# Scores of the last eight attention units: two insertions of 32-row matmuls become one of 64-row matmuls, with halves of q and k moved between row groups by ScalarE copies

## The chip, the cores and the metric

The kernel runs on one core of a Trainium2 chip. The metric is device time in microseconds (us): the median of the executions of one program. A profiled execution gives a trace of each engine: TensorE (PE for matmuls, PEld for the loads of their stationary operand), VectorE (DVE), ScalarE (ACT), GpSimd (POOL), and SyncE (SP), which issues most of the loads. ScalarE issues DMAs too (ACTq).

## The reference

Three layers in a row, all in float32: attention within chunks of 64 positions, an RMS norm with a gated MLP (512 to 1536 to 512), and a second MLP (512 to 2048 to 512). There are 8 x 576 = 4608 tokens of 8 heads x 64.

```python
def _attn_ref(q, k, v):                       # (8, 8, 576, 64) each
    scores = scale * np.matmul(q_c, k_c.transpose(0, 1, 2, 4, 3))
    scores = scores - np.max(scores, axis=-1, keepdims=True)
    attn = np.exp(scores)
    attn = attn / (np.sum(attn, axis=-1, keepdims=True) + 1e-09)
    out = np.matmul(attn, v_c)
...
def _moe_ref(x, w_gate, w_val, w_out, rms_g):
    xn = x / np.sqrt(np.mean(x * x, axis=-1, keepdims=True) + 1e-06) * rms_g
    g = xn @ w_gate
    silu = g * (1.0 / (1.0 + np.exp(-g)))
    return silu * (xn @ w_val) @ w_out
...
def _moe2_ref(x, w_in, w_out):
    h = x @ w_in
    return (h * np.clip(h + 3.0, 0.0, 6.0) / 6.0) @ w_out
```

## The kernel before

**Stages.** The 4608 tokens are nine blocks of 512. The first stage computes the first MLP for blocks 0 to 2; the second (it begins at 379 us) does it for blocks 3 to 8, two blocks at a time; the third is the second MLP. Every large matmul is made of three matmuls on a high and a low part of the operands: the high part is a ScalarE cast (a "cast" below), the low part a VectorE or GpSimd subtraction of it from the original.

**A pair of blocks in the second stage.** A pair first goes through the *product part*. Its gate and value matrices are multiplied by a scheme of seven products of sums and differences of blocks in place of eight. The products of one group of hidden columns are written as slots (pr, m): product pr from 1 to 7 and half m, 0 or 1. A slot is six matmuls of `product` (line 1034 in the trace). The order of slots in a group is (1,0), (1,1), then (4,·) and (3,·) of the group before, (5,·) and (6,·), and at the end (2,0), (7,0), (2,1), (7,1). The first group has no (4,·) and (3,·). The accumulation banks of a group are read ("evacuated") behind certain slots:
- (6,0) and (6,1): ScalarE copies, lines 1433 and 1436. These are the two evacuations that the prediction speaks of ahead of the activation.
- (2,0): ScalarE's Silu activation, line 1353. Slot (1,0) of the next group overwrites the bank that it reads.
- (7,0): a ScalarE copy (1444), a VectorE addition, and a Silu after the next slot. (7,1): a ScalarE copy (1449) and a VectorE addition.
- (2,1): a VectorE multiply on the bank (line 1362 as all of these additions and multiplies): the "late multiply". Slot (1,1) of the next group overwrites that bank.

After six groups the *second part* of the pair follows: 24 items of 12 matmuls each by w_out (`mm_down_a`), whose operands are split by a ScalarE cast and a GpSimd subtraction (lines 1357 and 1358) two items ahead.

**Attention in between.** While one pair is computed, the attention of the following blocks is put in between. A unit of attention is 256 tokens of all heads. The second stage has eight (`Wide`, indices 10 to 17), four under each of the first two pairs. Unit n of a pair begins at 0, 14, 28 or 42 ticks after the pair's start; a pair has 66 ticks. A *tick* is two slots (12 matmuls, 2.74 us at the spacing of the trace) or one item. At each tick the kernel's own agenda (`at`, `tick`) runs the steps that are due then, so each engine's order of instructions is the order in which the program's lines run. The steps and their ticks are in the table `STEPS_P` (line 43). Units 1 and 5 begin in their pair's first group: `turn_q` is run behind slot (1,1), `turn_k` behind (5,1), and steps of ticks 2 and 3 behind (6,1) and (2,1) (this group ends with (2,0), (2,1), (7,0), (7,1)). Units 2, 3, 6 and 7 begin in a later group: `turn_q` behind (3,1), `turn_k` behind (6,0), and steps of ticks 2 and 3 behind (6,1) and (7,0). What is due at tick 5 lies behind the first slots of the group that follows.

**The steps of a unit.** `turn_q` and `turn_k` are one VectorE transpose of 32 x 32 blocks each (`turned`, line 908; 128 rows x 1024 elements). Of a head's 64 features, the transposed tile holds features 0 to 31 of a head (g = 0) in one half of its columns and 32 to 63 (g = 1) in the other half, on the same 32 rows. So a score, a sum over 64 features, is two accumulating matmuls on 32 rows (`start=g == 0`, `stop=g == 1`). `scores0` and `scores1` insert 32 such calls each between product matmuls; in the trace a call counts as two records, line 928. `top0` and `top1` take the maxima (VectorE, line 939), then come `less`, `expo`, `total`, `share`, a transpose of the result, `values`, and the squares for the norm.

The units of the first stage (`Pair`, the base class) have q and k loaded in another layout and make their scores in one insertion of 32 calls on 64 rows (line 799).

**Beside the units** the same queues hold: the sums and differences of the block operands (VectorE, lines 1252 and 1248, and ScalarE casts 1245, "xt" and "xu"); a preparation of weights for the third stage (`Raw`: loads "sraw" issued on ScalarE's queue, line 248; an activation, VectorE bit operations 256, 257, 262, 265; the cast of line 277 to "shi" or "sc"; the subtraction 278 on GpSimd; and stores to a stash, lines 296 and 300, on ScalarE's queue); and the RMS norm of a finished block (lines 957 to 984), which falls into units 3 and 7.

**Temporaries.** xt, sc, shi, slo and s3 share one pool, `tmp_p`, of four buffers of 128 x 512, taken in turn. A tile that takes a buffer waits until everything that uses the buffer's tile before is done.

## Time and profile before

| What | Value |
|---|---|
| Median of three runs | 1682.11 us (1678.25, 1682.11, 1682.73) |
| Profiled execution | 1679.51 us |
| Its span in the trace | 1677.7 us |
| TensorE matmuls | 1649.2 us, 98% of the span, 9920 records |
| VectorE | 1086.8 us, 65% |
| ScalarE | 845.2 us, 50% |
| GpSimd | 459.5 us, 27% |
| Mean granted TensorE clock | 0.995 of full speed |

The span is the time from the first to the last instruction in the trace; the execution's own time is 1.8 us longer. A timeline row gives a start, a duration, the engine and the program's line; in brackets stands how long the engine had stood idle before it, and which instruction released it. Rows of the same kind that follow each other are joined, and "x" counts them. Matmuls overlap, so the spacing of starts tells what one of them costs TensorE, not its duration.

### The profile page before, as it was taken

Reading aid. Unit: us, or ns where it says so; the run is one execution under the profiler, and the core shown is the slowest. Engines: PE = TensorE matmul, PEld = TensorE weight load, DVE = VectorE, ACT = ScalarE, POOL = GpSimd, SP = SyncE. Lnnn points to the kernel's source line nnn. Section 1 sums busy time; section 2 is a strip of 40 time slices with the busy share of each in tenths; the row PEclk is TensorE's granted clock in tenths of the full one; section 3 lists DMA queues with packets and bytes.
Section 4 is the critical chain, followed back from the end, with each engine's and each line's share of the span. In section 5 each row is a group of like instructions: output and inputs, shape, how many; then the busy total and the mean of one; then the engine's idle time right before and its main releaser. Section 6 shows DMA issues by size and latency. Waiting matters only on the chain.

```text
span 1677.7 us, 26541 instructions
## 1 busy us (share of the span) xinstructions
PE 1649.2 (98%) x9920; PEld 1350.7 (81%) x9920; DVE 1086.8 (65%) x1600; ACT 845.2 (50%) x1409; POOL 459.5 (27%) x336
## 2 busy tenths in 40 slices
PE   8999999999999999999999999999999999999998
PEld 7777888878878888788887888888788878887886
DVE  6998566656575775758436378448746764874475
ACT  6786344455454454645434344455445544654552
POOL 1001434321326522364226622131023003301310
PEclk8999999999999999999999999999999999999999
DMA  9913777747876488855979766667767786777665
GB/s 301 271 37 71 207 208 222 205 152 251 292 262 224 168 297 286 290 176 185 361 238 316 293 239 226 213 190 250 219 209 224 209 243 191 223 218 235 189 200 150
DMA packets 336096, 375.07 MB, mean 224 GB/s; under 512 B 184288, under 2 KB 260064, under 8 KB 335840
## 3 DMA queue, kind: packets, MB, share of 16 engines
q1 hardware_dynamic: 273984, 302.84, 58.4%
q10 hardware_dynamic: 61984, 70.53, 12.2%
q8 instruction: 79, 1.29, 0.3%
q14 instruction: 49, 0.40, 0.1%
HBM read 292.55 MB, written 80.74 MB: 223 GB/s over the span
## 4 chain that ended last, share of the span: by engine, by line
PE 45%; DVE 5%; DMA 1%; ACT 1%; issue 1%; SPq 1%; DVEq 0%; POOL 0%; ACTq 0%; POOLq 0%
PE PS L1034 24%; PE PS L1584 13%; PE PS L1023 2%; DVE gs L1578 1%; PE PS L1051 1%; PE PS L1048 1%; PE PS L1049 1%; DVE gt L1720 1%; PE PS L1056 1%; PE PS L1057 1%; PE PS L1060 1%; SPq L1603 1%; DMA stash_in<-sc 1%; PE PS L1784 1%; DVE oq L1598 0%
## 5 line engine op out<-in xcount | busy, mean ns | idle before, releaser
L1034 PE MATMUL PS<-xu,wo 128*128 128x512 f32 x1512 | 353.1, 392 | 3.4 <-DVE gu L1362 2.3
L1034 PEld LDWEIGHTS PS<-xu,wo 128*128 128x128 f32 x1512 | 282.3, 188 | 65.0 <-DVE gu L1362 3.1
L1034 PE MATMUL PS<-xo,wq 128*128 128x512 f32 x1344 | 305.3, 389 | 0.0
L1584 PE MATMUL PS<-gs,wq 128*128 128x512 f32 x1296 | 296.2, 390 | 2.4 <-DVE gs L1578 2.0
L1034 PEld LDWEIGHTS PS<-xo,wq 128*128 128x128 f32 x1344 | 252.3, 188 | 52.4
L1584 PEld LDWEIGHTS PS<-gs,wq 128*128 128x128 f32 x1296 | 242.7, 188 | 55.3 <-DVE gs L1578 5.0
L1023 PE MATMUL PS<-XH,w 128*128 128x512 f32 x576 | 148.9, 401 | 5.1 <-ACT sg L1331 3.1
L1023 PEld LDWEIGHTS PS<-XH,w 128*128 128x128 f32 x576 | 108.0, 191 | 29.2 <-ACT sg L1331 3.8
L1048 PE MATMUL PS<-gs,wd 128*128 128x512 f32 x288 | 113.4, 394 | 1.6 <-DVE gu L1362 1.6
L1049 PE MATMUL PS<-gs,wd 128*128 128x512 f32 x288 | 112.2, 390 | 0.0
L1079 POOL TENSOR_TENSOR al<-sg,ah 128x512 fp32r<-128x512 f32 x40 | 56.2, 1404 | 156.2 <-ACT ah L1077 151.9
L1358 POOL TENSOR_TENSOR gs<-gu,gs 128x512 fp32r<-128x512 f32 x60 | 86.6, 1461 | 42.7 <-ACT gs L1357 33.9
L1651 POOL TENSOR_TENSOR gt<-gx 128x512 f32<-128x512 f32 x8 | 10.3, 1289 | 299.8 <-DVE gx L1648 299.8
L1362 DVE TENSOR_TENSOR gu<-gu,PS 128x512 f32<-128x512 f32 x60 | 41.0, 685 | 77.4 <-ACT gu L1444 42.0
L1578 DVE TENSOR_TENSOR gs<-gu,gs 128x512 fp32r<-128x512 f32 x88 | 67.9, 792 | 31.4 <-ACT gs L1577 31.1
L1577 ACT CAST gs<-gt 128x512 fp32r<-128x512 f32 x96 | 58.3, 623 | 49.6 <-DVE gt L1720 44.3
L1515 DVE SCALAR_TENSOR_TENSOR gu<-gu,PS 128x512 f32<-128x512 f32 x48 | 32.8, 684 | 72.6 <-ACT gu L1512 72.6
L1023 PE MATMUL PS<-XL,w 128*128 128x512 f32 x288 | 78.9, 396 | 0.0
L1077 ACT CAST ah<-sg 128x512 fp32r<-128x512 f32 x52 | 32.3, 621 | 88.9 <-DVE sg L1335 63.2
L1051 PE MATMUL PS<-gs,wd 128*128 128x512 f32 x288 | 77.0, 389 | 0.0
L1577 ACT CAST gs<-gu 128x512 fp32r<-128x512 f32 x96 | 57.2, 621 | 22.8 <-DVE gs L1578 15.6
L1651 POOL TENSOR_TENSOR gt<-gu 128x512 f32<-128x512 f32 x24 | 32.5, 1355 | 129.0 <-DVE gu L1648 124.9
(251 smaller groups left out, 2887.6 us busy)
## 6 DMA issues: line engine op xcount, KB each, us to landing
wq<-stash_in SPq DMA_DIRECT2D x128, 512.0 KB
wo<-ops SPq DMA_DIRECT2D x126, 512.0 KB
wq<-sums_out SPq DMA_DIRECT2D x64, 512.0 KB
wq<-stash_out SPq DMA_DIRECT2D x48, 512.0 KB
wd<-keep_out SPq DMA_DIRECT2D x36, 512.0 KB
yd<-yst SPq DMA_DIRECT2D x18, 512.0 KB
ops<-w ACTq DMA_DIRECT2D x36, 256.0 KB
v<-in_v_dram SPq DMA_DIRECT2D x32, 256.0 KB
```

The lines of the kernel that those rows point to most:

```text
L1023: nc.tensor.matmul(ps, w(wi, c), xs[c][xi], start=(i == 0), stop=(i == n - 1))
L1034: nc.tensor.matmul(PS[:, bank, :], op[:, wi, c * 128:(c + 1) * 128], x[xi][:, c, :], start=first and i == 0, stop=last and i == 5, skip_gr ...
L1048: nc.tensor.matmul(ps, wm[0], a[0], start=first, stop=False)
L1049: nc.tensor.matmul(ps, wm[1], a[0], start=False, stop=False)
L1051: nc.tensor.matmul(PS[:, banks[m], :], w[:, 0, m * 128:(m + 1) * 128], a[1], start=False, stop=last)
L1079: nc.gpsimd.tensor_tensor(lo, t, hi.bitcast(F32), op=ALU.subtract)
L1358: nc.gpsimd.tensor_tensor(w[:, 1, :], t, w[:, 0, :].bitcast(F32), op=ALU.subtract)
L1362: nc.vector.tensor_tensor(o, x, y, op=op)
L1577: nc.scalar.copy(w[:, 0, :], x)
L1578: e.tensor_tensor(w[:, 1, :], x, w[:, 0, :].bitcast(F32), op=ALU.subtract)
L1584: nc.tensor.matmul(PS[:, banks[m], :], op[:, wi, m * 128:(m + 1) * 128], x[xi], start=first and (wi, xi) == (0, 0), stop=False, skip_group ...
L1651: nc.gpsimd.tensor_tensor(slot(i, "t"), slot(i, "12"), slot(i, "11"), op=ALU.subtract)
```

## The change

In the eight units a head's halves g = 0 and g = 1 are put on 64 neighbouring rows, so that a score is one matmul on 64 rows.

- `turned` makes three transposes of 128 x 512 in place of one of 128 x 1024: g = 1 into the second half of the target's columns, g = 0 into the first half, and g = 0 again into a new tile `half` from the pool `tmp_p`.
- `move_q` and `move_k` (new steps, ticks 2 and 3 of a unit) then make four ScalarE copies of 32 rows x 512 each: for each 64-row group, the lower rows' g = 1 goes to the upper rows' first half of columns, and the upper rows' g = 0 (from `half`, since that place in the target has just been overwritten) goes to the lower rows' second half.
- `scores` is one step at tick 5 (before, two steps at ticks 3 and 5): 32 calls on 64 rows. `top` is one maximum over all heads (that of the class `Pair`, line 809), in place of two over half of them.

The diff:

```diff
@@ -43,8 +43,9 @@
 STEPS_P = (
     (0, ("turn_q",)),
     (1, ("turn_k",)),
-    (3, ("scores0", "top0")),
-    (5, ("scores1", "top1")),
+    (2, ("move_q",)),
+    (3, ("move_k",)),
+    (5, ("scores", "top")),
     (6, ("less",)),
     (7, ("expo",)),
     (9, ("total", "share")),
@@ -905,43 +906,46 @@
                         yield
 
         def turned(self, to, x):
-            nc.vector.transpose(
-                out=to.rearrange("p (h g t u) -> p h u g t", h=2, g=2, u=8),
-                in_=x.rearrange("p (h u g f) -> p h u g f", h=2, u=8, g=2),
-            )
-
-        def scores(self, e):
+            self.moved = tmp_p.tile([128, 512], F32, tag="tmp", name="half")
+            for o, g in ((to[:, 512:1024], 1), (to[:, 0:512], 0), (self.moved, 0)):
+                nc.vector.transpose(
+                    out=o.rearrange("p (h t u) -> p h u t", h=2, u=8),
+                    in_=x.rearrange("p (h u g f) -> p h u g f", h=2, u=8, g=2)[:, :, :, g],
+                )
+
+        def move(self, to, moved):
+            for j in range(2):
+                lo, hi = slice(j * 64, j * 64 + 32), slice(j * 64 + 32, (j + 1) * 64)
+                nc.scalar.copy(to[hi, 0:512], to[lo, 512:1024])
+                nc.scalar.copy(to[lo, 512:1024], moved[hi, :])
+
+        def turn_q(self):
+            super().turn_q()
+            self.moved_q = self.moved
+
+        def move_q(self):
+            self.move(self.qT, self.moved_q)
+
+        def move_k(self):
+            self.move(self.kT, self.moved)
+
+        def scores(self):
             ps = PS[:, ATT:ATT + 2, :].rearrange("p z (t e c k) -> p z t e c k", t=2, e=2, c=2)
             self.s = PS[:, ATT:ATT + 2, :].rearrange("p z (x k) -> p z x k", k=CH)
             qT, kT = (
-                x.rearrange("p (h g n) -> p g h n", h=2, g=2) for x in (self.qT, self.kT)
+                x.rearrange("p (e h t c n) -> p h e t c n", e=2, h=2, t=2, c=2) for x in (self.qT, self.kT)
             )
             for t in range(2):
-                for y in range(2):
-                    for g in range(2):
-                        for h in range(2):
-                            for j in range(2):
-                                c = h ^ y
-                                f = slice((2 * j + e) * 32, (2 * j + e + 1) * 32)
-                                n = slice((2 * t + c) * 64, (2 * t + c + 1) * 64)
-                                x = side(2 * h + e, j)
-                                nc.tensor.matmul(
-                                    ps[x * 64:(x + 1) * 64, h, t, e, c, :],
-                                    qT[f, g, h, n],
-                                    kT[f, g, h, n],
-                                    start=g == 0,
-                                    stop=g == 1,
-                                )
-
-        def top(self, e):
-            if e == 0:
-                self.mx = sm_p.tile([128, 2, 2 * NP], F32, tag="mx", name="mx")
-            nc.vector.tensor_reduce(
-                out=self.mx.rearrange("p z (t e c) -> p z t e c", t=2, e=2)[:, :, :, e],
-                in_=self.s.rearrange("p z (t e c) k -> p z t e c k", t=2, e=2)[:, :, :, e],
-                axis=AX.X,
-                op=ALU.max,
-            )
+                for a, c, j in FOURS:
+                    f = slice(j * 64, (j + 1) * 64)
+                    x = side(a, j)
+                    nc.tensor.matmul(
+                        ps[x * 64:(x + 1) * 64, a // 2, t, a % 2, c, :],
+                        qT[f, a // 2, a % 2, t, c, :],
+                        kT[f, a // 2, a % 2, t, c, :],
+                        start=True,
+                        stop=True,
+                    )
 
     XN = {}
 
```

In what follows, the lines of the changed kernel stand 1 to 4 further down than those of before.

VectorE, the first ticks of unit 5, before (1252 and 1248 make operands, 908 is the turn, 1362 the late multiply, 939 the maximum):

```order
L1252 TENSOR_TENSOR xt<-xf 128x512
L908 STREAM_TRANSPOSE qT<-q 128x2x8x64
L1248 TENSOR_TENSOR xu<-xt,xu 128x512
L1252 TENSOR_TENSOR xt<-xf 128x512
L908 STREAM_TRANSPOSE kT<-k 128x2x8x64
L1248 TENSOR_TENSOR xu<-xt,xu 128x512 x2
L256 TENSOR_SCALAR sc<-sc 128x512
L257 TENSOR_SCALAR sc<-sc 128x512
L1362 TENSOR_TENSOR ge<-ge,PS 128x512
L939 TENSOR_REDUCE mx<-PS 128x4x2
```

VectorE, the same place, after:

```order
L1256 TENSOR_TENSOR xt<-xf 128x512
L911 STREAM_TRANSPOSE qT<-q 128x2x8x32 x2
L911 STREAM_TRANSPOSE half<-q 128x2x8x32
L1252 TENSOR_TENSOR xu<-xt,xu 128x512
L1256 TENSOR_TENSOR xt<-xf 128x512
L911 STREAM_TRANSPOSE kT<-k 128x2x8x32 x2
L911 STREAM_TRANSPOSE half<-k 128x2x8x32
L1252 TENSOR_TENSOR xu<-xt,xu 128x512 x2
L257 TENSOR_SCALAR sc<-sc 128x512
L258 TENSOR_SCALAR sc<-sc 128x512
L1366 TENSOR_TENSOR ge<-ge,PS 128x512
```

Each turn has become three transposes in a row, and the maximum (939) behind the multiply is gone from here.

ScalarE at unit 5, before, with what each row waits for by semaphore (1433 and 1436 are the evacuations of (6,0) and (6,1), 1353 the activation of (2,0), 255 an activation of the weights' preparation):

```order
L1245 CAST xu<-xt 128x512 [waits DVE_49] x2
L277 CAST shi<-sraw 128x512 [waits DMAHW6_49,DMAHW5_49]
L248 DMA sraw<-in_moe_w_out_dram 128x1024 [waits DMAHW1_49]
L1433 COPY gu<-PS 128x512 [waits PE_49]
L1436 COPY s_6104<-PS 128x512 [waits PE_49]
L1245 CAST xu<-xf 128x512
L255 ACTIVATE sc<-sraw 128x512 [waits DMAHW7_49,DMAHW2_49,DVE_49]
L1353 ACT_TABLE_LOAD
L1353 ACTIVATE ge<-PS 128x512 [waits PE_49]
```

ScalarE, the same place, after:

```order
L1249 CAST xu<-xt 128x512 [waits DVE_49] x2
L278 CAST shi<-sraw 128x512 [waits DMAHW7_49,DVE_49]
L249 DMA sraw<-in_moe_w_out_dram 128x1024 [waits DMAHW2_49]
L1437 COPY gu<-PS 128x512 [waits PE_49]
L1440 COPY s_6034<-PS 128x512 [waits PE_49]
L919 COPY qT<-qT 32x512
L920 COPY qT<-half 32x512 [waits Activation_49]
L919 COPY qT<-qT 32x512
L920 COPY qT<-half 32x512 [waits Activation_49]
L1249 CAST xu<-xf 128x512
L256 ACTIVATE sc<-sraw 128x512 [waits DMAHW3_49,Activation_49]
L1357 ACT_TABLE_LOAD
```

The four copies of `move_q` stand between the evacuation 1440 and the cast of an operand, ahead of the activation of (2,0), whose table load is the last row here. The cast `shi` now waits for a semaphore of VectorE.

ScalarE at unit 7, before (965 is the norm's square root, 300 the stores to the stash, 1444 the copy of (7,0)):

```order
L965 ACT_TABLE_LOAD
L965 ACTIVATE rt<-PS,eps 128x512 [waits PE_49]
L300 DMA stash_out<-sc 128x2x256 [waits DMAHW7_49,Activation_49]
L300 DMA stash_out<-slo 128x2x256 [waits DMAHW0_49,Pool_49]
L1353 ACT_TABLE_LOAD [waits DMAHW2_49]
L1353 ACTIVATE gu<-PS 128x512 [waits PE_49]
L1444 COPY gu<-PS 128x512 [waits PE_49]
```

ScalarE, the same place, after:

```order
L301 DMA stash_out<-sc 128x2x256 [waits DMAHW6_49,Activation_49]
L301 DMA stash_out<-slo 128x2x256 [waits DMAHW0_49,Pool_49]
L919 COPY qT<-qT 32x512 [waits DVE_49]
L920 COPY qT<-half 32x512 [waits DVE_49,Activation_49]
L919 COPY qT<-qT 32x512
L920 COPY qT<-half 32x512 [waits Activation_49]
L1357 ACT_TABLE_LOAD [waits DMAHW2_49]
L1357 ACTIVATE gu<-PS 128x512 [waits PE_49]
L1448 COPY gu<-PS 128x512 [waits PE_49]
L919 COPY kT<-kT 32x512 [waits DVE_49]
L920 COPY kT<-half 32x512 [waits DVE_49,Activation_49]
```

Here `move_q` stands directly ahead of the activation of (2,0), and `move_k` behind the copy of (7,0).

## Rows read from the trace of the kernel before

**Rows 1.** The page: busy time of each engine (share of span), instructions.
```profile
PE 1649.2 (98%) x9920; PEld 1350.7 (81%) x9920; DVE 1086.8 (65%) x1600; ACT 845.2 (50%) x1409; POOL 459.5 (27%) x336
```

**Rows 2.** Groups of tile kT: duration ns minimum/median/maximum, first to last start, forms.
```profile
L928 PE MATMUL PS<-kT,qT x1024: 217/217/361, 390.3 to 734.5; 32*64 32x64 f32 x171
...
L908 DVE STREAM_TRANSPOSE kT<-k x8: 2130/2144/2211, 384.7 to 721.9; 128x1024 f32<-128x1024 f32 x8
```

**Rows 3.** Timeline, TensorE, unit 1: start us, us, engine, line, tiles, count [idle <-releaser].
```profile
379.30 11.04 PE L1034 MATMUL PS<-xu,wo 128*128 128x512 f32 x48
390.27 1.16 PE L928 MATMUL PS<-kT,qT 32*64 32x64 f32 x64
391.36 5.73 PE L1034 MATMUL PS<-xu,wo 128*128 128x512 f32 x24
397.03 1.16 PE L928 MATMUL PS<-kT,qT 32*64 32x64 f32 x64
```

**Rows 4.** Timeline of TensorE at an earlier unit, in the first stage.
```profile
163.26 1.16 PE L799 MATMUL PS<-kT,qT 64*64 64x64 f32 x64
164.35 1.89 PE L1023 MATMUL PS<-XH,w 128*128 128x512 f32 x7
```

**Rows 5.** Timeline of VectorE (DVE) and ScalarE (ACT) at unit 1.
```profile
380.33 2.12 DVE L908 STREAM_TRANSPOSE qT<-q 128x1024 f32<-128x1024 f32 x1
...
382.28 0.69 DVE L1248 TENSOR_TENSOR xu<-xt,xu 128x512 fp32r<-128x512 f32 x1
...
384.69 2.13 DVE L908 STREAM_TRANSPOSE kT<-k 128x1024 f32<-128x1024 f32 x1
...
387.97 0.62 ACT L1245 CAST xu<-xt 128x512 fp32r<-128x512 f32 x1 [2.54 <-DVE xt L1252]
...
390.71 0.61 ACT L1353 ACTIVATE ge<-PS 128x512 f32<-128x512 f32 x1
```

**Rows 6.** Timeline of all engines at unit 5.
```profile
592.78 0.62 ACT L1245 CAST xu<-xt 128x512 fp32r<-128x512 f32 x1 [2.55 <-DVE xt L1252]
...
593.15 0.35 ACTq L248 DMA_DIRECT2D sraw<-in_moe_w_out_dram  x1
...
593.30 0.66 ACT L277 CAST shi<-sraw 128x512 fp32r<-128x512 f32 x1
...
594.65 1.87 DVE L1248 TENSOR_TENSOR xu<-xt,xu 128x512 fp32r<-128x512 f32 x2
...
595.95 0.69 ACT L255 ACTIVATE sc<-sraw 128x512 f32<-128x512 f32 x1 [0.50 <-DVE xu L1248]
...
596.49 5.73 PE L1034 MATMUL PS<-xu,wo 128*128 128x512 f32 x24
...
597.95 0.60 ACT L1353 ACTIVATE ge<-PS 128x512 f32<-128x512 f32 x1
...
601.72 0.62 ACT L1245 CAST xu<-xf 128x512 fp32r<-128x512 f32 x1 [3.17 <-DMA sraw<-in_moe_w_out_dram]
```

**Rows 7.** Timeline of all engines at unit 3.
```profile
474.37 0.37 ACTq L300 DMA_DIRECT2D stash_out<-sc  x1
...
478.85 0.65 ACT L277 CAST sc<-sraw 128x512 fp32r<-128x512 f32 x1 [2.38 <-DVE sraw L265]
...
485.49 2.93 PE L1034 MATMUL PS<-xu,wo 128*128 128x512 f32 x6 [2.26 <-DVE gu L1362]
```

**Rows 8.** Windows, unit 3: us, busy (count) of PE, PEld, DVE, ACT, POOL, PEclk, DMA, GB/s.
```profile
485.50:488.40 2.90, 2.90 (x10) 1.88 (x10) 2.87 (x3) 0.00 (x0) 1.66 (x1) 0.50 0.95 326
```

**Rows 9.** Timeline of all engines at unit 7.
```profile
683.17 0.60 ACT L1353 ACTIVATE gu<-PS 128x512 f32<-128x512 f32 x1
...
686.54 0.65 DVE L939 TENSOR_REDUCE mx<-PS 128x8 f32<-128x512 f32 x1
...
687.12 0.67 DVE L1362 TENSOR_TENSOR gu<-gu,PS 128x512 f32<-128x512 f32 x1
...
687.84 1.23 PEld L1034 LDWEIGHTS PS<-xu,wo 128*128 128x128 f32 x6 [0.45 <-DVE gu L1362]
```

## The prediction

> **What bounds the kernel now.** I read the page first: TensorE is busy for 98% of the span [rows 1], and the chain of waits that ends last is for the most part its own matmuls. So a time changes here only where TensorE gets less to do or waits more. Then I read the list of TensorE's waits over the stretch of the eight units: it waits a few times, for VectorE's multiplies and transposes, and never there for a DMA. Last I read the timeline of all engines at each of the eight places where a unit's q and k are turned. I number the units 1 to 8, 1 to 4 under the first pair of token blocks, 5 to 8 under the second. Units 1, 2, 3, 5, 6, 7 lie in the product part of their pair and units 4 and 8 in its second part (the multiplications by w_out).
>
> **What is taken from TensorE.** A unit's scores are now two insertions of 64 records of 32 rows x 64 columns [rows 2]; each takes 390.27 to 391.36, 1.09 us [rows 3]. An insertion costs a little more than its length: 48 product matmuls in a row go at 10.97/48 = 0.2285 us, and the 24 between two insertions take 5.67 instead of 5.48 us, 0.19 more [rows 3]. The new insertion is 32 calls where there were 64, so again 64 records, now of 64 rows x 64 columns. The earlier units run just that form: 163.26 to 164.35, 1.09 us [rows 4]. So a unit saves one insertion, 1.28 us, and eight save 10.2 us.
>
> [...]
>
> **What is added on VectorE.** A turn of 1024 elements keeps VectorE from 380.33 to 382.28, 1.95 us [rows 5], twice per unit. It becomes three pieces of 512, about 1.0 us each by half of that, 3.05 us: +1.1 per turn, +2.2 once both are past. One of the two maxima over half a unit leaves the place before the late multiply (0.6 us from start to start, 686.54 to 687.12 in [rows 9]).
>
> **What is added on ScalarE.** Eight copies of 32 rows x 512 elements per unit, in two blocks of four. No row shows a ScalarE copy on 32 rows. The nearest rows are 128 x 512 casts and copies, 0.58 to 0.66 us [rows 6]; they are the upper end. A quarter of that, if the time went with the rows, is the lower end. I take the upper end, since the elements per row are the same; the copies overlap a little and the second of a pair waits for the first, so a block is 2.4 us (lower end 0.6). [...]
>
> These blocks stand in ScalarE's queue, and not at a free place: block q stands ahead of the activation of product (2,0), block k ahead of the copy of (7,0) or just behind it. TensorE may start (1,0) of the next group, which overwrites that bank, only when the activation has read it.
>
> *Unit 1.* The cast at 387.97 had stood idle 2.54 us for VectorE [rows 5], so it moves by the two turns, +2.2. Behind it come the two evacuations, block q (+2.4) and the activation, which ended at 390.71 + 0.61 = 391.3. It now ends at 395.9. TensorE began (1,0) at 391.36 + 12 x 0.2285 = 394.1 [rows 3]. So +1.8 us, with the insertion that is gone already counted, as it is wherever I compare times of TensorE.
>
> *Unit 5.* The same, and worse. The temporary that the cast shi takes was free before; in the new allocation it is one that VectorE still reads in the first of the two subtractions at 594.65 [rows 6], behind both turns. That ends at 595.3, now +2.2 = 597.5, so shi starts there and not at 593.30: +4.2. Block q adds 2.4; the 0.5 us for which the row at 595.95 waited for VectorE goes. The activation ended at 598.55 and now ends 6.1 later, at 604.6; TensorE began (1,0) at 596.49 + 2.74 = 599.2 [rows 6]. So +5.4 us.
>
> *Unit 3.* The normalization stands in the same queues. ScalarE idled 2.38 us before the cast at 478.85, for VectorE, and block q fits into that. VectorE's +2.2 goes through cast, table load, activation and copy to the multiply for which TensorE waited 2.26 us at 485.49 [rows 7]; the maximum ahead of that multiply is gone, -0.6. So +1.6 us. The third piece of k also waits for a store of the stash, issued at 474.37 [rows 7], because it takes the temporary that this store reads. VectorE comes there about 4.1 us after the issue. What such a store takes no row shows; the nearest, a load of twice the size issued at 593.15, let go of ScalarE at 601.72, 8.6 us later [rows 6]. So between 0 and 4.5 us more; I take 0, since it is half the size, and keep the rest for the range.
>
> *Unit 7.* Here ScalarE does not idle, so block q goes straight into the chain that ends with TensorE's wait at 687.84: the activation at 683.17 moves by 2.4, the multiply by 2.4 - 0.6 [rows 9]. So +1.8 us.
>
> *Units 2 and 6.* By the same queues the activation comes in time there, and the late multiply comes between in time and one insertion late: between -1.3 and 0, and I take the middle, -0.7 each. *Units 4 and 8.* In the second part of a pair TensorE waits for casts and subtractions that are made two items (some 5.5 us) ahead, and that covers a block: -1.3 each. If that cover is gone, a block costs up to 2.4.
>
> Other queues: the new waits on SyncE (the next unit's q and k may be loaded only after the third piece, 1.1 us later) hold the product operands queued behind them, which are loaded several products ahead; I cost them at nothing, at most 1.1 us a unit.
>
> **The sum.** +1.8 + 5.4 + 1.6 + 1.8 - 2 x 0.7 - 2 x 1.3 = +6.6 us. [...] Unit 5 will stand idle twice for some 3 us, and I count one such loss: +8.0 us in all. Against the profiled execution, 1679.5 us, that is 1687.5; the median of the three runs shown is 2.6 above it, and 1682.1 + 8.0 = 1690.1.
>
> **The rivals.**
> - *The side engines hide all of it.* For it: ScalarE is busy half of the time and VectorE two thirds. Against it: the rows above, where ScalarE or VectorE is late already. It would give 1682.1 - 10.2 = 1671.9. It decides where the copies are short and the queue finds room before (1,0).
> - *The copies go with the rows.* A block is 0.6 us. Unit 1 comes to 0, unit 5 to +3.6, unit 7 to 0, unit 3 stays at +1.6, and the others bring -5.2: 0 in all, 1682.
> - *Worse than my sum.* Unit 3's piece of k waits for its store (+4.5), and the clock falls in units 1 and 7 as well (+1.4 each): +15.3, 1697.4. For it: VectorE has 65% of its time taken, and stores from ScalarE's queue share the DMA engines with TensorE's operands.
> - *64 rows take twice as long.* 8 x 1.28 us come on top: 1700.3. The measured form speaks against it.
>
> **How the numbers follow.** My forecast, 1686 to 1694: 0.44. Everything hidden: 0.12. Short copies, or half of the delay: 0.24. Worse: 0.18. Twice as long: 0.02. A measurement of this kernel can tell some 0.3%, 5 us, from no change. Faster by more than that: 0.13 (all hidden, and a little of the second). Within: 0.24. Slower: 0.63. The range is 1674 to 1702: it leaves out most of the first rival and the end of the worse ones. The forecast's own range is 1686 to 1694.
>
> **What would show it.** Right: one insertion of 64 records of some 1.09 us per unit; three transposes of about 1.0 us; ScalarE copies of 0.55 to 0.65 us on 32 rows; waits of TensorE for an activation or its PSUM read in units 1 and 5, some 3 us at a time, with a half clock behind; the cast shi of unit 5 idle for VectorE; a wait of VectorE for stash_out in unit 3 only if it is the worse case. Wrong: no new waits of TensorE in these units and copies of a quarter of the time (then the kernel is as fast or faster), or an insertion of 2 us.

## The result and the profile after

The changed kernel takes 1691.72 us (median of four runs, 1690.67 to 1693.07) against 1680.18 us for the kernel before (four runs). The ratio is 1.0069, with a 95% interval of 1.0049 to 1.0088: 11.5 us slower. The profiled execution took 1691.26 us, its span is 1689.4 us, 11.7 more than before.

The page of the changed kernel, busy time of each engine, answers to [rows 1]:

```profile
PE 1645.4 (97%) x9408; PEld 1346.6 (80%) x9408; DVE 1100.6 (65%) x1624; ACT 884.7 (52%) x1473; POOL 459.6 (27%) x336
```

TensorE has 512 records less, 8 x 64, so the saved insertions are there. ScalarE has 64 instructions more and 39.5 us more work, VectorE 24 more and 13.8 us. TensorE's busy time fell by 3.8 us only, because some of what is left ran at a lower clock (the 1512 matmuls of `product` on xu and wo take 357.9 us, where they took 353.1); the span grew although it fell, so TensorE stood idle longer.

The groups of tile kT after the change (duration in ns, minimum/median/maximum; first to last start; forms) answer to [rows 2]:

```profile
L942 PE MATMUL PS<-kT,qT x512: 217/219/367, 398.2 to 746.4; 64*64 64x64 f32 x171
L911 DVE STREAM_TRANSPOSE kT<-k x16: 1107/1146/1190, 384.7 to 737.0; 128x512 f32<-128x512 f32 x16
L919 ACT COPY kT<-kT x16: 613/617/624, 395.2 to 740.2; 32x512 f32<-32x512 f32 x16
L920 ACT COPY kT<-half x16: 613/617/619, 395.9 to 740.8; 32x512 f32<-32x512 f32 x16
```

A record on 64 rows takes 219 ns as one on 32 rows took 217. A ScalarE copy on 32 rows takes 0.617 us, and its copies of 128 x 512 from the accumulation banks take 0.57 to 0.59 in the same trace: fewer rows did not shorten it.

What TensorE waits for in the stretch of the units (us in total, times, longest). Before, this list had 2.3 us for one late multiply and nothing else over 1.2:

```profile
PE PS L1038 <- ACT gu L1357: 5.0, 2, 3.7
PE PS L1038 <- ACT ge L1357: 4.9, 2, 3.2
PE PS L1038 <- DVE gu L1366: 3.9, 4, 1.8
PE PS L1038 <- ACT gu L1437: 2.9, 1, 2.9
PE PS L1038 <- DVE s L1366: 2.0, 1, 2.0
...
```

The new waits are for ScalarE's activation of (2,0) (line 1357), for the evacuation of (6,0) (line 1437), and for VectorE's multiplies and additions (line 1366).

To see where the time goes I take from both traces the start of each unit's `values` matmuls. Before they start at 420.99, 464.23, 512.55, 555.47, 626.70, 669.62, 714.56 and 757.48 us, after at 423.28, 465.76, 516.53, 558.14, 637.00, 679.70, 727.78 and 769.39. The stage itself begins at 379.30 before and at 378.36 after: the first stage, which the change doesn't touch, ran 0.9 us faster in this execution. A unit's own part is how much the difference grows over it. Unit 5's end, before and after:

```profile
626.70 1.16 PE L855 MATMUL PS<-qT,v 64*64 64x64 f32 x64
```

```profile
637.00 1.16 PE L856 MATMUL PS<-qT,v 64*64 64x64 f32 x64
```

The parts of all units:

| Unit | 1 | 2 | 3 | 4 | 5 | 6 | 7 | 8 | sum |
|---|---|---|---|---|---|---|---|---|---|
| Predicted, us | +1.8 | -0.7 | +1.6 | -1.3 | +6.8 | -0.7 | +1.8 | -1.3 | +8.0 |
| Measured, us | +3.2 | -0.8 | +2.5 | -1.3 | +7.6 | -0.2 | +3.1 | -1.3 | +12.8 |

(The prediction's 1.4 us for the clock stands in unit 5.) The sum less the 0.9 is the 11.7 of the span, to 0.2.

Unit 5 after, from the timeline of all engines, answers to [rows 6]; each row is start, duration, engine, line, tiles, and in brackets the idle time and its releaser:

```profile
599.88 0.66 ACT L278 CAST shi<-sraw 128x512 fp32r<-128x512 f32 x1 [2.87 <-DVE xu L1252]
...
601.08 3.01 PE L1038 MATMUL PS<-xu,wo 128*128 128x512 f32 x12 [2.93 <-ACT gu L1437]
601.54 0.62 ACT L919 COPY qT<-qT 32x512 f32<-32x512 f32 x1
...
603.47 0.62 ACT L920 COPY qT<-half 32x512 f32<-32x512 f32 x1
...
606.60 0.60 ACT L1357 ACTIVATE ge<-PS 128x512 f32<-128x512 f32 x1
...
607.25 5.49 PE L1038 MATMUL PS<-xu,wo 128*128 128x512 f32 x12 [3.16 <-ACT ge L1357]
```

The cast shi stands idle for VectorE, the evacuation of (6,0) comes behind it and TensorE waits 2.93 us for that; then come the four copies, 601.54 to 604.09, and TensorE waits 3.16 us more for the activation. Its next twelve matmuls take 5.49 us, twice the usual 2.74.

Windows of the changed kernel (us, busy and count of PE, PEld, DVE, ACT, POOL, then PEclk, DMA, GB/s), the first in unit 5, the others in unit 3, answer to [rows 8]:

```profile
607.30:612.70 5.40, 5.40 (x16) 3.79 (x16) 3.21 (x5) 4.54 (x9) 0.00 (x0) 0.50 0.46 149
485.10:488.40 3.30, 2.85 (x6) 1.74 (x6) 2.85 (x5) 3.18 (x6) 0.00 (x0) 0.50 0.56 115
...
491.40:493.30 1.90, 1.90 (x65) 1.78 (x65) 0.80 (x1) 0.00 (x0) 0.26 (x1) 0.50 0.58 203
```

The granted clock is 0.50 of full speed in unit 5 for 5.4 us and in unit 3 from 485.1 to 493.3, where before it was so from 485.5 to 488.4.

### The profile page after: what moved, and what is told of

Read it like the earlier page. It is cut to its first block, busy times and chain, and to the rows that moved or that the text cites. A ratio compares the mean times of both kernels' runs of the same rounds, so it can differ in the third digit from the quotient of the medians.

```text
span 1689.4 us, 25596 instructions
## 1 busy us (share of the span) xinstructions
PE 1645.4 (97%) x9408; PEld 1346.6 (80%) x9408; DVE 1100.6 (65%) x1624; ACT 884.7 (52%) x1473; POOL 459.6 (27%) x336
## 4 chain that ended last, share of the span: by engine, by line
PE 76%; DVE 12%; ACT 4%; DMA 3%; issue 2%; SPq 2%; POOL 0%; ACTq 0%; DVEq 0%; POOLq 0%
PE PS L1038 33%; PE PS L1588 13%; PE PS L1027 9%; PE PS L1052 5%; PE PS L1055 5%; PE PS L1053 5%; DVE gs L1582 1%; DMA wo<-ops 1%; PE PS L856 1%; DVE wtmp L186 1%; DVE gt L1724 1%; PE PS L1060 1%; PE PS L1061 1%; PE PS L1064 1%; DVE w L206 1%
## 5 line engine op out<-in xcount | busy, mean ns | idle before, releaser
L1038 PE MATMUL PS<-xu,wo 128*128 128x512 f32 x1512 | 357.9, 396 | 19.8 <-ACT gu L1357 5.0
```

The costliest lines, as they stand in the source:

```text
L1038: nc.tensor.matmul(PS[:, bank, :], op[:, wi, c * 128:(c + 1) * 128], x[xi][:, c, :], start=first and i == 0, stop=last and i == 5, skip_gr ...
```

## The experiments

The times of all kernels here are compared with the kernel before as run beside them. The units' own parts are worked out as above, one execution each; units 4 and 8, where nothing happens but the saved insertion, come out between -1.30 and -1.31 in nearly all, while the start of the stage moves by up to 1.7 us between executions, so the ratio of the runs and the parts of the units are read together.

| Kernel | ratio (95%) | 1 | 2 | 3 | 4 | 5 | 6 | 7 | 8 |
|---|---|---|---|---|---|---|---|---|---|
| changed kernel | 1.0069 (1.0049, 1.0088) | +3.2 | -0.8 | +2.5 | -1.3 | +7.6 | -0.2 | +3.1 | -1.3 |
| e1 scores only | 0.9944 (0.9924, 0.9963) | -1.3 | -1.6 | -2.0 | -1.3 | +1.1 | -1.3 | -0.3 | -1.3 |
| e2 three turns | 0.9978 (0.9967, 0.9990) | +0.1 | -1.6 | +2.4 | -1.3 | +0.3 | -1.1 | +0.1 | -1.3 |
| e4 GpSimd | 1.0034 (1.0021, 1.0047) | +1.7 | -1.3 | +0.3 | -1.3 | +7.5 | -0.5 | -0.3 | -1.3 |
| e10 own half | 1.0047 (1.0032, 1.0061) | +3.1 | +0.2 | +1.9 | -1.3 | +3.5 | -0.2 | +3.2 | -1.3 |
| e11 own half, GpSimd | 0.9987 (0.9975, 0.9999) | +0.0 | -1.3 | +2.6 | -1.3 | +0.9 | -0.4 | -0.3 | -1.3 |
| e13 even units | 0.9969 (0.9958, 0.9979) | +0.1 | -1.3 | -1.4 | -1.3 | +0.8 | -0.5 | -0.0 | -1.3 |

**Scores alone (e1).** One transpose per turn as before, no copies, no tile half:

```diff
-    (2, ("move_q",)),
-    (3, ("move_k",)),
...
-            for o, g in ((to[:, 512:1024], 1), (to[:, 0:512], 0), (self.moved, 0)):
+            nc.vector.transpose(
+                out=to.rearrange("p (h g t u) -> p h u g t", h=2, g=2, u=8),
```

> This kernel leaves out the three pieces of each turn and all the copies: one transpose of 1024 as before, and the new scores (one insertion of 32 calls on 64 rows, one maximum). It multiplies rows that don't belong together, for the time alone. Theory (the new scores are worth one insertion per unit, everything lost is lost by the side engines): 8 x 1.28 = 10.2 us below the kernel before, some 1670 us, and no wait of TensorE that the kernel before has not. Rival (an insertion of 64 rows costs TensorE as much as two of 32 rows, or scores at one tick bring a wait of their own): within 3 us of the kernel before.

Measured: 1672.21 us against 1680.34, ratio 0.9944. The 64-row insertion does save its twin; the rival of equal cost is out. Of the 10.2 us some 8 to 9 arrive; the theory's other half, no new wait of TensorE, did not hold. In units 5 and 7 less of it arrives than elsewhere: TensorE comes sooner to what the side engines have not finished (in unit 5 it waits 1.18 us for a ScalarE copy and 0.40 for an operand).

**Three turns, no copies (e2).** The changed kernel without the steps `move_q` and `move_k`:

```diff
-    (2, ("move_q",)),
-    (3, ("move_k",)),
```

> The changed kernel without the eight copies (left out: the moves of halves between row groups, so the scores multiply wrong rows); the three transposes and the tile half are there. Theory (VectorE's longer turns count by themselves where a cast waits for VectorE, in units 1, 3 and 5): unit 3 stays at +1.6 and unit 5 at +3.0 us, the six others bring -1.3 each; together some -3 us, 1677 to 1680. Rival A (the copies on ScalarE are the whole loss): as the kernel with the new scores alone, some -10 us, 1670. Rival B (VectorE and the tile half are the whole loss): as the changed kernel, +11.6, 1692.

Measured: 1677.32 us, ratio 0.9978, -3 us, as the theory said, but not by its units: unit 5 lost 0.3 and not 3.0, and units 1 and 7 came to +0.1. Why unit 5 fell so far shows in its cast shi, from this kernel's timeline:

```profile
593.54 0.66 ACT L276 CAST shi<-sraw 128x512 fp32r<-128x512 f32 x1
```

It does not wait. The same tiles are asked for in the same order as in the changed kernel, so the four buffers are not simply taken in turn: here shi has got another one. That half is free earlier where no copy reads it is my reading; the trace shows no buffers. It was the first sign that part of unit 5's loss is the temporary's.

**Copies alone (e6).** The kernel before with eight copies of qT and kT onto themselves:

```diff
-    (3, ("scores0", "top0")),
+    (2, ("move_q",)),
+    (3, ("move_k", "scores0", "top0")),
```

> The kernel before with eight ScalarE copies of 32 rows x 512 per unit, each of a piece of qT or kT onto itself, at ticks 2 and 3; transposes, scores and maxima as before. Theory (a block of 2.56 us ahead of the activation of (2,0) counts where that activation has less room than this): units 5 and 7 lose about 2 us each, unit 2 and 6 up to 1.3, unit 1 and 3 nothing, as their VectorE is not later; +4 to +6 us, 1684 to 1688. Rival A (copies are hidden in ScalarE's idle half): 0. Rival B (copies are the whole loss): 10.2 + 11.6 = +22 us, 1702.

Measured: 1734.16 us, ratio 1.0305. No expectation held, and the reason is in the experiment: `scores0` is due at the tick of `move_k`, so TensorE waited for the copies themselves, as the list of its waits over the span shows:

```profile
PE PS L941 <- ACT kT L918: 37.0, 14, 8.0
```

It says nothing on the copies' place in ScalarE's queue, but it shows why the changed kernel has its scores two ticks later.

**Copies on GpSimd (e4).** In `move`:

```diff
-                nc.scalar.copy(to[hi, 0:512], to[lo, 512:1024])
-                nc.scalar.copy(to[lo, 512:1024], moved[hi, :])
+                nc.gpsimd.tensor_copy(to[hi, 0:512], to[lo, 512:1024])
+                nc.gpsimd.tensor_copy(to[lo, 512:1024], moved[hi, :])
```

> The changed kernel with the eight copies of a unit on GpSimd in place of ScalarE, at the same ticks. Theory (what is lost behind the copies is their place in ScalarE's queue): as the kernel without copies, some -3 us against before, if GpSimd copies 32 rows x 512 in some 1.3 us as it subtracts 128 x 512; two blocks then take 10.4 us and are through before the scores at tick 5 (13.7 us). Rival (the moves delay the scores wherever they run, or GpSimd is slower): TensorE waits at the scores for kT, up to some us per unit, and the time is that of the changed kernel or longer.

Measured: 1686.21 us, ratio 1.0034, between theory and rival, and TensorE has no wait for kT. Unit 7 falls from +3.1 to -0.3 and unit 1 by half, but unit 5 stays at +7.5, with not one copy on ScalarE. A row of its timeline, and one of its groups:

```profile
596.04 0.65 ACT L278 CAST shi<-sraw 128x512 fp32r<-128x512 f32 x1 [2.85 <-DVE xu L1252]
```

```profile
L920 POOL COPY qT<-half x16: 604/610/956, 383.0 to 731.1; 32x512 f32<-32x512 f32 x16
```

The cast waits for the temporary as in the changed kernel. And GpSimd copies in 0.61 us what ScalarE copies in 0.62.

**Half in the source tile (e5).** The third piece goes over columns of the source tile that are read by then:

```diff
-            self.moved = tmp_p.tile([128, 512], F32, tag="tmp", name="half")
...
+            nc.vector.transpose(out=xv[:, :, :, 1], in_=xv[:, :, :, 0])
+            self.moved = xv[:, :, :, 1]
```

> The changed kernel with the third piece of each turn written into the source tile (over its g = 1 columns, which are read by then) and not into a temporary, and the loads of the next unit's q and k asked for after move_k; copies on ScalarE at the same ticks. Theory (unit 5's loss of 7.6 us is mostly the wait of the cast shi for a temporary that VectorE still reads): unit 5 falls to some +2.5 us and the rest stays, so +5 to +6 us against before, 1685 to 1686. Rival (the copies' place in ScalarE's queue is the loss in unit 5 as well): as the changed kernel, +11.6, 1692.

Measured: 1692.23 us, ratio 1.0070, as the changed kernel. By the time alone the rival would win, but the timeline shows the cast shi without a wait, and the groups show what took its place:

```profile
596.17 0.66 ACT L278 CAST shi<-sraw 128x512 fp32r<-128x512 f32 x1
```

```profile
L918 ACT COPY kT<-kT x16: 613/617/621, 395.4 to 741.1; 32x512 f32<-32x512 f32 x16
L919 ACT COPY kT<-k x16: 1122/1163/1247, 396.0 to 741.7; 32x512 f32<-32x512 f32 x16
```

The copy from the source tile has to scatter its elements 32 bytes apart and takes 1.16 us instead of 0.62, so a block grew from 2.6 to 3.7 us. The experiment changed the temporary and the copies (and the time of the next loads) at once and decides nothing; e10 was made for that.

**One tick later (e7).** As e5, with the blocks behind the activation of (2,0):

```diff
-    (2, ("move_q",)),
-    (3, ("move_k",)),
+    (3, ("move_q",)),
+    (4, ("move_k",)),
```

> As e5_source, with the two blocks of copies one tick later (3 and 4 in place of 2 and 3), so that the block of q stands behind the activation of (2,0) and the block of k behind (7,1); scores still at tick 5. Theory (what the copies cost is their place ahead of an activation that TensorE needs at once): as the kernel without copies, -3 to -4 us, 1676 to 1678. Rival (a block of 2.56 us costs the same wherever it stands): as e5_source. A wait of TensorE for kT at the scores would show that the copies come too late.

Measured: 1709.35 us, ratio 1.0174 (1.0143, 1.0205). Neither theory nor rival: the copies come too late for the scores at tick 5.

```profile
PE PS L941 <- ACT kT L918: 19.7, 12, 4.3
```

With copies of 1.16 us there is no room behind the activation either: the place at ticks 2 and 3 costs an activation, the place at ticks 3 and 4 the scores. Copies of 0.62 us at ticks 3 and 4, or scores a tick later, were not run.

**Source tile and GpSimd (e8).** e5 with the copies on GpSimd, as in e4.

> As e5_source, with the copies on GpSimd at ticks 2 and 3. With the copies on GpSimd and the tile half in the pool of temporaries unit 5 still lost 7.5 us, as the cast shi stood waiting for VectorE. Theory (that wait is one for a temporary): unit 5 falls to some +0.3 us, as in the kernel without copies, and the whole to -3 to -4 us, 1676 to 1678. Rival (GpSimd's copies hold something else in unit 5): +5 to +6 as with the tile half.

Measured: 1685.30 us, ratio 1.0032 (1.0018, 1.0045). Unit 5 fell to +4.1 only. The scattered copies take 1.15 us on GpSimd too, and TensorE waited for them at the scores, 3.9 us in all:

```profile
PE PS L941 <- POOL kT L918: 2.5, 2, 1.7
PE PS L941 <- POOL kT L919: 1.4, 2, 0.7
```

**Swap on GpSimd without the third piece (e9).** One transpose of 1024 as before, and six copies per tensor:

```diff
+                nc.gpsimd.tensor_copy(moved[lo, 0:512], to[hi, 0:512])
+                nc.gpsimd.tensor_copy(to[hi, 0:512], to[lo, 512:1024])
+                nc.gpsimd.tensor_copy(to[lo, 512:1024], moved[lo, 0:512])
```

> One transpose of 1024 per turn as before (its target laid out by g), and the swap of halves by twelve GpSimd copies of 32 rows x 512 in place of eight, over the source tile; no third piece, no temporary, nothing new on ScalarE or VectorE. Theory (TensorE's saving is real and only the side engines' queues eat it): as the new scores alone, -9 to -10 us, 1671; GpSimd's two blocks of 6 x 0.65 us must be through by tick 5, 13.7 us after the turn of q. Rival (the swap is late, or GpSimd's subtractions behind it are): TensorE waits for kT at the scores, or for a split operand, and the gain is gone.

Measured: 1682.34 us, ratio 1.0011 (1.0000, 1.0023). VectorE and ScalarE have nothing new here, and still the gain is gone: twelve copies are not through by tick 5, and TensorE waited 5.4 us for kT in its insertions. That is the rival, but only about half of the 10 us by which it misses e1; the rest was not traced to a cause.

**Half in a pool of its own (e10).** One edit of the changed kernel:

```diff
-            self.moved = tmp_p.tile([128, 512], F32, tag="tmp", name="half")
+            self.moved = ah_p.tile([128, 512], F32, tag="ah", name="half")
```

> The changed kernel with one edit: the tile half comes from a pool that nothing uses in this stage, not from the pool of temporaries; copies of 0.62 us on ScalarE at ticks 2 and 3. (In e5_source the copies from the source tile took 1.16 us each, which hid what was asked.) Theory (unit 5's loss of 7.6 us is two things, the cast shi's wait for a temporary and a block of 2.56 us): shi no longer waits for VectorE, unit 5 falls to some +2.5 us, the other units stay; +6 to +8 us, 1686 to 1688. Rival (the temporaries cost nothing beside the block): unit 5 stays at 7 to 8, the whole at +11, 1691.

Measured: 1687.09 us, ratio 1.0047. The theory holds, with unit 5 at +3.5 for its +2.5: the cast shi no longer waits, unit 5 falls from +7.6 and the other units stay within 1 us. In unit 5 TensorE now waits 0.74 us for an operand and 1.76 for the activation, where it was 2.93 and 3.16:

```profile
597.61 0.65 ACT L278 CAST shi<-sraw 128x512 fp32r<-128x512 f32 x1
```

```profile
604.95 4.23 PE L1038 MATMUL PS<-xu,wo 128*128 128x512 f32 x12 [1.76 <-ACT ge L1357]
```

**The same with the copies on GpSimd (e11).** e10 with the lines of e4.

> As e10_own_half, with the copies on GpSimd at the same ticks (0.61 us each). Theory (what is then left of the loss is VectorE's third piece): as the kernel without copies, -3 to -4 us, 1676 to 1678, no wait of TensorE for kT, since 2 x 2.6 us of copies are through before tick 5. Rival (GpSimd's copies delay its subtractions, and these a cast or a multiply): within 2 us of before, with a wait for POOL in some chain.

Measured: 1678.19 us, ratio 0.9987, 1 us below the kernel before and 9 below e10. The time is a little above the theory's and inside the rival's. The rival's sign is there too: ScalarE's casts of the second part (line 1361) wait 6.5 us for slo and 4.0 for qT on GpSimd, where before they waited 2.7 for slo. But that does not reach TensorE: units 4 and 8 are at -1.3, and TensorE waits neither for kT nor for anything else of GpSimd. Units 1, 5 and 7 lose their ScalarE waits. It is within 1 us of the kernel without any copies (e2), or 2 where each is taken against the kernel before that ran beside it: GpSimd makes the copies for nearly nothing. What stays is unit 3, +2.6, as in e2 (+2.4), so it is there without any copy: VectorE's longer turns delay the chain to the activation, for which TensorE waits 4.0 us here and 3.7 in e2. But e4 has the same waits in unit 3 and comes to +0.3:

```profile
483.59 2.93 PE L1038 MATMUL PS<-xu,wo 128*128 128x512 f32 x6 [4.01 <-ACT gu L1357]
487.02 1.66 PE L1038 MATMUL PS<-xu,wo 128*128 128x512 f32 x6 [0.50 <-DVE gu L1366]
```

There six matmuls took 2.93 us, the next six 1.66 and the scores 1.16; in e2 and e11 both sixes took 2.93 and the scores 1.99. In e4 the clock was back after six matmuls, then, and in e2 and e11 only after twelve and the scores. So some 2 us of what stays in unit 3 are the clock's, and they come in one execution and not in another.

**An early swap with five copies (e12).** e9 with the copies directly behind the turns and one copy of 128 x 512 for two of 32 rows:

```diff
-    (0, ("turn_q",)),
-    (1, ("turn_k",)),
-    (2, ("move_q",)),
-    (3, ("move_k",)),
+    (0, ("turn_q", "move_q")),
+    (1, ("turn_k", "move_k")),
```

> As e9_swap_pool, with five GpSimd copies per tensor in place of six (one of 128 x 512 into the source tile, four of 32 x 512) and at ticks 0 and 1, directly behind the turns, so that GpSimd's other work is not ahead of them. In e9_swap_pool TensorE waited 5.4 us for kT. Theory (the saving is real where nothing new stands on ScalarE and VectorE and the swap is in time): no wait for kT, as the new scores alone, -8 to -10 us, 1670 to 1672. Rival (GpSimd's queue is then late for its subtractions): the gain is smaller, with waits for slo or a stash store.

Measured: 1694.36 us, ratio 1.0072 (1.0045, 1.0099). TensorE no longer waits for kT, but GpSimd's queue stands behind VectorE's turns, and in units 4 and 8 (+4.5 and +3.3) TensorE waits for the operands that GpSimd subtracts:

```profile
PE PS L1053 <- POOL gs L1360: 7.6, 4, 3.3
```

The rival's way, and further than it said.

**The even units alone (e13).** The new form in units 2, 4, 6 and 8 as in e11, the old one in units 1, 3, 5 and 7:

```diff
+    class Wide64(Wide):
...
-        unit = [(Pair if i < 10 else Wide)(i) for i in range(NPR)]
+        unit = [(Pair if i < 10 else Wide64 if i % 2 else Wide)(i) for i in range(NPR)]
```

> The new form only in units 2, 4, 6 and 8, with the tile half in the unused pool and the copies on GpSimd as in e11_own_half_pool; units 1, 3, 5 and 7, which start a pair or coincide with the norm, stay as in the kernel before. Theory (each unit's loss is that of its own place, so the units can be put together from the runs): -1.3, -1.3, -0.4 and -1.3 us as these units had in e11_own_half_pool, -4.3 us in all, some 1675.5, faster than both. Rival (a unit's change is carried into the next one and only the sum over all of them counts): as e11_own_half_pool, within 2 us of the kernel before.

Measured over five rounds: 1674.55 us against 1679.84, ratio 0.9969 with an interval of 0.9958 to 0.9979. It beats both kernels. The parts of the units are those of e11 in the even ones, -4.4 in all, as the theory has it, and, but for unit 3's -1.4, within 0.8 us of nothing in the odd ones. In unit 3 six matmuls took 1.65 us and not 2.93 in the profiled execution, so the clock stayed high (see the end), which the theory did not count; without it the parts make -3.6 and not -5.1.

**Where the 11.5 us come from.** The medians of the chain e1, e2, e10 and the changed kernel make a sum: the new scores -8.1 (1672.21 - 1680.34), the three pieces +5.1 (1677.32 - 1672.21), the copies in ScalarE's queue +9.8 (1687.09 - 1677.32), half among the temporaries +4.6 (1691.72 - 1687.09). The third step is not one edit, as e2 still has half among the temporaries; but its cast shi does not wait, and e10 against e11, which is one edit, gives 8.9 for the copies' place. The two losses are not independent: with half among the temporaries the copies' place is worth 5.5 (changed kernel against e4), and with the copies on GpSimd the temporaries are worth 8.0 (e4 against e11). So the split is that of this order of steps. A median of this kernel moves by about 1 us between the groups of runs, so each term holds to about 2.

## Why the prediction was right, point by point

**TensorE's saving.** 1.28 us per unit, from the two forms' equal 1.09 us [rows 3, 4]: units 4 and 8 show -1.3 each, and e1 -8 in all. The rival of twice the time is out.

**VectorE's turns.** Three pieces of some 1.0 us were predicted: in unit 1 they take 379.43 to 382.37, 2.94 us. The 3.05 of the prediction does not follow from its own half of 1.95 us, which gives 2.93 for three pieces; the 0.1 us changes nothing.

**ScalarE's copies.** The upper end, 0.58 to 0.66 us, was taken and 0.617 came; a block of four takes 2.55 us, 2.4 were estimated. The rival of copies that go with the rows is out by this row alone.

**Unit 5.** I compare the start of (1,0), which waits for the activation, counted from unit 4's `values`. Before: 596.49 + 2.74 - 555.47 = 43.8. After: 607.25 - 558.14 = 49.1. So +5.35, where +5.4 stood, and by the very steps: the cast shi waits for VectorE until 599.88, then the block, then the activation. The cast shi itself starts 41.7 us behind `values` (599.88 - 558.14) and not 37.8 (593.30 - 555.47): +3.9, predicted +4.2. The prediction gave all of that to the temporary. In e10, without it, shi still starts 38.8 us behind (597.61 - 558.80), so the temporary makes 2.9 of it, and 1.0 comes from VectorE's longer turn of q through the cast ahead of shi. That unit 5 as a whole falls by 4.2 us in e10 is the clock again: (1,0) starts 3.0 us sooner (604.95 - 558.80 = 46.15), and its twelve matmuls take 4.2 us and not 5.4. The half clock behind it stands in the sum with 1.4 us, a term that no run shows: in unit 3 of the kernel before six matmuls took 2.93 us at a granted 0.50 [rows 7, 8], where six at 0.2285 us take 1.37. Here twelve took 607.25 to 612.67, 5.42 us at 0.50, against 2.92 before, so it cost 2.5.

**Unit 1.** (1,0) stood 14.8 us behind the start of the stage before (394.1 - 379.30) and 16.9 after (395.23 - 378.36): +2.1, predicted +1.8. Two signs that the prediction gave did not come here: TensorE waits 1.69 us for the activation and not some 3, and there is no half clock behind it. The rest of the +3.2 comes a group later. TensorE's rows of unit 1 after:

```profile
383.08 10.46 PE L1038 MATMUL PS<-xu,wo 128*128 128x512 f32 x43 [0.71 <-DVE xu L1252]
395.23 3.01 PE L1038 MATMUL PS<-xu,wo 128*128 128x512 f32 x12 [1.69 <-ACT ge L1357]
...
405.82 11.20 PE L1038 MATMUL PS<-xu,wo 128*128 128x512 f32 x48 [0.82 <-DVE gu L1366]
```

The last wait, 0.82 us, is for a VectorE multiply behind the scores. VectorE is late there because it stood idle for ScalarE's copy of (7,0), 1.89 us where it was 0.44 before. A row from before and one from after:

```profile
393.67 0.69 DVE L1362 TENSOR_TENSOR gu<-gu,PS 128x512 f32<-128x512 f32 x1 [0.44 <-ACT gu L1444]
```

```profile
398.39 0.69 DVE L1366 TENSOR_TENSOR gu<-gu,PS 128x512 f32<-128x512 f32 x1 [1.89 <-ACT gu L1448]
```

The four copies of kT, 395.20 to 397.74, stand directly ahead of that copy. The prediction named this place of block k and gave it no cost. In e2, e4 and e11, with the same three pieces on VectorE but no copies on ScalarE, unit 1 does not have this wait.

**Unit 7.** The late multiply lets (1,1) start 10.8 us behind the norm's matmul (699.90 - 689.09) and not 8.8 (687.85 - 679.01): +2.0, predicted +1.8. Again there is a second wait, a group later, 2.03 us where the kernel before had 0.86. The first two rows are the norm's matmul before and after:

```profile
679.01 0.40 PE L962 MATMUL PS<-sqh,ones_r 128*128 128x512 f32 x1
```

```profile
689.09 0.40 PE L966 MATMUL PS<-sqh,ones_r 128*128 128x512 f32 x1
...
699.90 1.66 PE L1038 MATMUL PS<-xu,wo 128*128 128x512 f32 x6 [1.78 <-DVE gu L1366]
...
713.06 8.46 PE L1038 MATMUL PS<-xu,wo 128*128 128x512 f32 x36 [2.03 <-DVE s L1366]
```

That is the other +1.2 of this unit. In e11, with the copies on GpSimd, the second wait is 1.11 us, and in e2 0.66, so it too comes from the copies' place on ScalarE. No run has block q without block k, so how much of it is either's stays open.

**Unit 3.** The place predicted is the late multiply: (1,1) starts 13.3 us behind the norm's matmul (488.46 - 475.15) and not 11.9 (485.49 - 473.63), +1.45 where +1.6 stood. The wait for a store of the stash, kept for the range, did not come: half of k is turned at 479.97, with no idle time ahead. But now the activation is late as well, so that TensorE waits 3.75 us ahead of (1,0) and 0.50 ahead of (1,1), and the clock stays low until 493.3, which costs the other 1.0. The norm's matmul before, then the rows after:

```profile
473.63 0.40 PE L962 MATMUL PS<-sqh,ones_r 128*128 128x512 f32 x1
```

```profile
475.15 0.40 PE L966 MATMUL PS<-sqh,ones_r 128*128 128x512 f32 x1
...
485.03 2.93 PE L1038 MATMUL PS<-xu,wo 128*128 128x512 f32 x6 [3.75 <-ACT gu L1357]
...
488.46 2.93 PE L1038 MATMUL PS<-xu,wo 128*128 128x512 f32 x6 [0.50 <-DVE gu L1366]
491.32 1.99 PE L942 MATMUL PS<-kT,qT 64*64 64x64 f32 x64
```

Before, unit 3 had the low clock too, from 485.5 to 488.4 [rows 8]; the prediction counts nothing for its lasting longer.

**Units 2, 6, 4 and 8** came as predicted, to 0.5 us.

So in units 1, 3, 5 and 7 the slot that the prediction named comes late by what it said, to within 0.3 us, and the time, 1691.72, lies in its likeliest case, 1686 to 1694. The sum of +8.0 was too small by 4.8 us in the units. Two terms are mis-sized, both in the same way: what follows the first wait. The copies' block of k and the late ScalarE queue behind it, in units 1 and 7 (1.1 and 1.2 us), which the prediction put at nothing without a reason, and the clock in units 5 and 3 (1.1 and 1.0 us). The small remainders of the predicted waits make up the rest. That the forecast of 1690.1 came so near is luck: it was counted from a median of 1682.1, while four runs give 1680.2 for the kernel before. From there the same sum gives 1688.2, still inside the forecast but 3.5 us short.

**Could it have been better?** The loss is not in the 64-row scores. In the order of the sum above it is VectorE's pieces, 5 us, the copies' place in ScalarE's queue, 10, and the temporary, 5. e11 shows the change without the last two, and e13 that it pays where nothing else is late.

## What to carry to other kernels

A saving on the engine that bounds a kernel is worth what the side engines' queues leave of it: follow the queue that gets the new work to the bank or buffer that the bounding engine needs next, and then one group further, since a late queue stays late there (units 1 and 7). A new tile in a rotating pool changes who waits for whom in code that the edit doesn't touch; give it a pool that is idle there, and look at the waits of the other users of the pool. Where units of work fall into different places of a schedule, cost each place by itself: the same change can be worth -1.3 us in one and +7.6 in another, and be kept only where it pays.

## What the runs showed of the hardware

**Copies and rows.** On ScalarE a copy of 512 elements took about the same on 32 rows as on 128: 0.617 us for 32 x 512 beside 0.57 to 0.59 for 128 x 512 copies from the accumulation banks and 0.62 for 128 x 512 casts such as xu<-xt. GpSimd made the copies of 32 x 512 in 0.61 us (e4); its subtractions of 128 x 512 took 1.3 to 1.5 (changed kernel). In unit 1 of e12 its copies of 128 x 512 took 0.92 and 2.06 us, beside 0.60 to 0.98 for those of 32 x 512.

**Scattered writes.** A copy whose writes lie 32 bytes apart took 1.16 us on ScalarE (e5) and 1.15 on GpSimd (e8), against 0.62 and 0.61 in a row. VectorE's transposes show the same. In e5 the piece that writes runs of 32 elements took 0.70 us, and the pieces that scatter by 32 bytes 1.17, at equal size:

```profile
L911 DVE STREAM_TRANSPOSE qT<-q x16: 1120/1170/1279, 379.4 to 733.7; 128x512 f32<-128x512 f32 x16
...
L912 DVE STREAM_TRANSPOSE q<-q x8: 672/703/715, 381.4 to 734.6; 128x512 f32<-128x512 f32 x8
```

So the scattered writes of 512 elements cost some 0.5 us more on each of the three engines: 0.54, 0.54 and 0.47. Other distances were not run, and no run shows the cause.

**VectorE beside GpSimd.** In e12, while GpSimd's copies run one behind the other, VectorE's subtractions take 1.09 us and not 0.68, and GpSimd's copies 0.95 and not 0.61:

```profile
382.64 1.09 DVE L1254 TENSOR_TENSOR xt<-xw,xt 128x512 f32<-128x512 f32 x1
...
383.25 0.95 POOL L917 COPY qT<-qT 32x512 f32<-32x512 f32 x1
383.66 1.09 DVE L1250 TENSOR_TENSOR xu<-xt,xu 128x512 fp32r<-128x512 f32 x1
```

The rows show both engines slowed by 0.3 to 0.4 us an instruction while they run side by side; by what, no run shows.

**The clock.** How long TensorE stood idle does not by itself tell whether the clock falls. In the kernel before a wait of 2.26 us was followed by a granted clock of 0.50 [rows 7, 8]; in e13 the same place had the same wait and six matmuls then took 1.65 us, where they took 2.93 in the kernel before:

```profile
483.93 1.65 PE L1088 MATMUL PS<-xu,wo 128*128 128x512 f32 x6 [2.26 <-DVE gu L1416]
```

In the changed kernel a wait of 2.93 us (601.08) was followed by twelve matmuls in 3.01 us (granted 1.00 from 601.1 to 604.1), and the wait of 3.16 us behind them by twelve in 5.49 (granted 0.50 from 607.3 to 612.7). What decides stays open.
